# Attention with memory and a gated FFN on one core: a new hand-listed order of all work

## The chip, the cores and the metric

The kernel runs on one core of one Trainium2 chip. The metric is the device time of one execution in microseconds (us), as the median of several runs; a separate, profiled execution gives the trace. The core's engines are PE (matrix multiplication), DVE (vector), ACT (activation functions and copies with scale), POOL (a second, general vector engine) and SP, which here only issues DMA transfers. Each engine works through its own list of instructions in order, and they meet through semaphores.

## The reference

Both halves read the same tokens `x` (2048 tokens of width 512). One half is causal-style attention in four segments of 512 tokens with 32 heads of width 16, plus a linear memory that each segment reads and then adds to. The other half is a gated feed-forward network of width 1792. A gate per token mixes them.

```python
q, k, v = x @ wq, x @ wk, x @ wv            # 32 heads, 4 segments of 512
mask = (ar[:, None] < ar[None, :]) * -1e9
for s in range(4):
    p = softmax(qs @ ks.T * Dh**-0.5 + mask); a_dot = p @ vs
    a_mem = (phi(qs) @ M) / (phi(qs) @ z + 1e-6)      # phi(t) = t + 1 if t > 0 else exp(t)
    o = sigmoid(beta) * a_mem + (1 - sigmoid(beta)) * a_dot
    M, z = M + phi(ks).T @ vs, z + sum(phi(ks))
a = o @ wo
b = (gelu(x @ w_gate) * (x @ w_up)) @ w_down
g = sigmoid((x * gate_w).sum(-1))
return g * a + (1 - g) * b
```

## The kernel before

The work is cut into 1020 named tasks. A task is a run of instructions on one engine, and its name holds the segment `s` first: `K0_1` is the key product of segment 0, block 1. The names that matter here:

- `ld_...`: loads. `ld_x0_*`, `ld_x1_*`, `ld_x2_*` bring the tokens of a segment, from segment 1 on as four transposing DMAs of 128 KB, one slice of 128 of the 512 columns each. `ld_wk*`, `ld_wq*`, `ld_wv`, `ld_wg*`, `ld_wu*`, `ld_wd*`, `ld_wo` bring weights: `ld_wg0` and `ld_wg0b` are the two halves (448 KB each) of the gate weight's first seven blocks, `ld_wg1` the other seven blocks (896 KB), `ld_wu0`, `ld_wu1`, `ld_wd0`, `ld_wd1` 896 KB each, `ld_wv` 512 KB. `ld_x0_1`, `ld_wk0` and `ld_wg0b` are issued by ACT, all others by SP. `ld_beta` brings `beta` to all partitions.
- `xtr0_*`, `xev0_*`: the first 256 tokens are transposed on PE and evicted. `K`, `Q`, `V`, `G`, `U`: products (`dense`, L449; V at L499; segment 0's K at L477) of four matmuls, each group into one of four PSUM banks `psD`. A colon and a digit behind a PE task's name is its bank. `Kev`, `Qev`, `Vev`, `Gev`: their evictions, on ACT (`:a`) or DVE (`:d`). `h` multiplies U into the gelu of G. A `G` product's four matmuls take the four slices of x one after another.
- `st`, `exp`, `msk`: a fill of scores into `psX` (L602), its exp on ACT (L609), its mask on POOL (L615). There is one `psX`, so a fill waits for the exp before it. `pv` (L644) is the product with the values, `tp` and `pvp` its turning and scaling on DVE.
- `vsh` and `ktr`: DMAs on SP from SBUF to SBUF that shift values by 64 partitions and transpose keys for the memory; `mz`, `nd`, `ndp`, `otr`, `ota`, `otm`: the memory's write and read.
- `betab`, `bexp`, `gqa`, `gqb`: the gate of the heads from `beta`, on DVE, ACT, POOL, DVE. `phka`, `phkb`, `phkc`: phi of the keys on DVE, ACT, DVE.
- `out` (L735), `wev`, `wo` (L749), `oev` (L753), `dma`: the down product, the output product, their mix and the store of 128 tokens.

What stands where is set by one string, `ORDER`: it lists all tasks, and an engine's list of instructions is the tasks of that engine in the string's order. The string also picks the bank of each PE product and the engine of each eviction. Nothing is decided at run time; the semaphore waits follow from which task reads and writes what.

```python
for word in ORDER.split():
    name, _, how = word.partition(":")
    t = by[name]
    ...
    if t.opens:
        for sl, i in zip(t.slots, how):
            sl.i = int(i)
```

Some loads also wait for others by hand: `ld_wv` for `ld_x0_t3`, `ld_wg0` and `ld_wu0` for `ld_wq1`, all four `ld_x1_*` for `ld_wv`, `ld_wu1` for `ld_wg0`, `ld_x2_*` for `ld_wu1`, `ld_wo` for `ld_wu0`. `ld_wd0` waits for nothing, and `ld_wg1` for nothing when it is listed ahead of `ld_wu0`.

Of the kernel before, what the change touches and what calls it, by code (L numbers as in the profile page):

```python
# [878 lines left out]
exp1_0A st1_0B exp1_0B tp0_d20 tp0_d21 pvp0_20 tp0_d30 ota0_1 pvp0_21 tp0_d31 kpada1_3 out0_1_0:1 out0_1_1 out0_1_2 V2_0a:2 Vev2_0a:d G1_9:3 V2_1b:0
Vev2_1b:d wev0_1:d st1_0C G1_8:2 G1_10:0 G1_11:1 gelu1 gd1_9 G1_7:3 gd1_8 gd1_10 gd1_7 gd1_11 G1_13:2 gd1_13 G1_12:0 gd1_12 phqc1_2 phkc1_0 mzq0  # L880
pvp0_31 pvp0_30 ota0_3 V2_0b:3 Vev2_0b:d ota0_2 V2_1a:1 Vev2_1a:d out0_0_0:2 out0_0_1 out0_0_2 nd1_0:0 ndp1_0 phkc1_2 exp1_0C st1_0D exp1_0D K2_0:3
K2_2:1 wev0_0:d Kev2_0:d Kev2_2:a K2_1:0 st1_0E Kev2_1:d U1_2:2 h1_2 wo0_1:1 nd1_3:3 nd1_1:0 exp1_0E st1_1A ld_x3_2 vsh1_00 vsh2_01 ktr1_1 ktr1_0
oev0_1 ndp1_1 wo0_0:2 oev0_0 kpada2_0 vsh1_21 out0_2_0:1 nd1_2:0 msk1_0C msk1_0A exp1_1A st1_1B exp1_1B msk1_0B gz1 msk1_0E msk1_1A msk1_0D msk1_1B
out0_2_1 wo0_2:2 ndp1_2 st1_1C exp1_1C nd1_5:0 out0_2_2 ndp1_3 wev0_2:a ndp1_5 out0_3_0:3 st1_1D nd1_4:0 out0_3_1 out0_3_2 ktr1_2 dma0 vsh1_01 otr1_3
ndp1_4 otr1_0 oev0_2 phka2_0 msk1_1C wev0_3:d ktr1_3 dma1 vsh2_00 otr1_1 ld_x3_1 ld_x3_0 ld_x3_3 exp1_1D st1_2A exp1_2A gr1 msk1_1D pv1_1:1023 st1_2B
exp1_2B tp1_d01 tp1_d00 kpadb1_3 V2_2b:0 Vev2_2b:d K2_3:1 Kev2_3:a G2_3:0 pvp1_00 Gev2_3:d tp1_d10 st1_2C U1_8:1 G2_1:0 otr1_2 V2_3a:2 h1_8 Gev2_1:d
Vev2_3a:d kpadb2_0 kpadb2_1 exp1_2C st1_2D phkb2_0 exp1_2D G2_6:1 wo0_3:0 U1_3:2 pvp1_01 tp1_d11 Gev2_6:a h1_3 phka2_2 oev0_3 st1_2E U1_0:3 V2_3b:1
G2_0:2 Gev2_0:d h1_0 Vev2_3b:d exp1_2E phkb2_2 st1_3A mz1:0 G2_4:2 G2_5:3 pvp1_10 mza1 Gev2_5:d exp1_3A st1_3B exp1_3B Gev2_4:d U1_11:1 G2_2:0
Gev2_2:d ota1_0 U1_13:3 h1_13 U1_10:2 h1_10 h1_11 G2_11:0 G2_10:3 pvp1_11 phkc2_0 phkc2_2 ota1_1 otm1_0 otm1_1 G2_12:2 G2_9:1 st1_3C gelu2 gd2_11
gd2_12 G2_7:0 G2_13:2 gd2_10 gd2_9 gd2_7 gd2_13 G2_8:3 gd2_8 U1_7:1 U2_9:0 K3_0:2 h1_7 U2_5:3 Q3_0:1 phqa2_0 h2_9 h2_5 Qev3_0:d Kev3_0:d exp1_3C  # L890
st1_3D exp1_3D U1_1:0 U2_12:3 msk1_3A msk1_2A msk1_3B U2_13:1 h2_12 h1_1 h2_13 kpada2_1 st2_0A U1_9:2 V2_2a:3 U2_7:0 msk1_2D msk1_2B msk1_2E h1_9
Vev2_2a:d vsh2_20 dma2 dma3 ktr2_0 ktr2_2 vsh2_21 exp2_0A phqb2_0 msk1_3D msk1_2C msk1_3C st2_0B h2_7 kpada2_2 pv1_3:1230 tp1_d21 exp2_0B tp1_d20
V3_1a:2 Vev3_1a:a st2_0C exp2_0C pvp1_21 tp1_d31 U1_6:1 Q3_1:2 V3_0a:0 st2_0D h1_6 pvp1_20 Vev3_0a:d Qev3_1:a V3_2b:1 U1_4:2 U1_5:0 exp2_0D st2_0E
exp2_0E tp1_d30 phqc2_0 h1_5 h1_4 ota1_2 Vev3_2b:a U1_12:3 h1_12 pvp1_31 pvp1_30 out1_1_0:0 st2_1A V3_1b:2 out1_1_1 V3_3a:3 exp2_1A st2_1B msk2_0B
msk2_0D Vev3_3a:a exp2_1B out1_1_2 U2_4:1 msk2_0E goa1 gob1 kpadb2_3 kpada2_3 msk2_0C msk2_0A msk2_1A ota1_3 h2_4 otm1_2 otm1_3 K3_1:3 mzq1 Vev3_1b:a
wev1_1:a st2_1C msk2_1B goc1 U2_1:2 Q3_3:1 V3_0b:0 Kev3_1:d kpada3_0 h2_1 Qev3_3:d kpadb2_2 exp2_1C msk2_1C st2_1D V3_2a:3 U2_6:2 exp2_1D Vev3_2a:a
wo1_1:1 Vev3_0b:d kpadb3_0 h2_6 oev1_1 st2_2A msk2_1D pv2_1:0231 exp2_2A st2_2B exp2_2B tp2_d00 pvp2_00 phqa2_2 tp2_d01 tp2_d10 pvp2_10 pvp2_01
tp2_d11 out1_0_0:0 out1_0_1 st2_2C phqb2_2 out1_0_2 V3_3b:2 Vev3_3b:d wev1_0:d out1_3_0:3 phqc2_2 pvp2_11 exp2_2C st2_2D exp2_2D wo1_0:1 out1_3_1
# [46 lines left out]
```

## Time and profile before

| what | value |
|---|---|
| time, median of 3 runs | 263.54 us (263.52 to 266.09) |
| the profiled execution's own time | 263.46 us |
| its span, from first to last instruction | 261.7 us |
| PE busy | 257.5 us, 2849 matmuls |
| DVE, ACT, POOL busy | 198.0, 203.2, 98.4 us |
| weight loads on PE (PEld) busy | 122.1 us |
| moved by DMA | 16.50 MB |

The profile is a page about one execution, with views behind it. The time is 1.76 us more than the span, which is what lies around the instructions. A matmul's busy time in the profile runs to a modelled end and overlaps the next one's, so starts one after another tell more than busy time. "Idle before" is time in which an engine stood still ahead of an instruction, with what ended it. DMA shares are means over the core's 16 DMA engines, and may stand above 1 where packets wait in flight.

### The profile page before, as it was taken

The numbers are of one execution on the slowest core, as the hardware profiler recorded it, in microseconds if no ns is written. First come the engines' busy times: TensorE is split into PE (matmuls) and PEld (weight loads), VectorE is DVE, ScalarE is ACT, GpSimd is POOL, SyncE is SP. The second block draws the span as 40 slices with busy tenths as digits, with TensorE's granted clock in tenths as the row PEclk, the third lists the DMA queues.
The fourth block names the chain that finished last, engine by engine and source line by source line (L and its number), as shares of the span: only waits on it lengthen the run. The fifth ranks groups of instructions, "written<-read, shape, count | busy, mean of one in ns | idle before, by whom it ended". The sixth has DMA issues, their size and how long they took to land.

```text
span 261.7 us, 6706 instructions
## 1 busy us (share of the span) xinstructions
PE 257.5 (98%) x2849; PEld 122.1 (47%) x2849; DVE 198.0 (76%) x412; ACT 203.2 (78%) x171; POOL 98.4 (38%) x163
## 2 busy tenths in 40 slices
...
DMA packets 31990, 16.50 MB, mean 63 GB/s; under 512 B 21592, under 2 KB 31960, under 8 KB 31960
## 3 DMA queue, kind: packets, MB, share of 16 engines
...
HBM read 7.87 MB, written 2.10 MB: 38 GB/s over the span
## 4 chain that ended last, share of the span: by engine, by line
PE 98%; DVE 0%; issue 0%; DVEq 0%
PE psD L449 48%; PE psD L735 19%; PE psX L602 9%; PE psD L644 6%; PE psD L499 6%; PE psD L749 5%; PE psD L477 1%; PE psD L547 1%; PE psD L383 1%; PE psD L577 1%; DVE xT L795 0%; DVE ost L753 0%; PE psX L786 0%; DVEq L818 0%; PE psD L769 0%
## 5 line engine op out<-in xcount | busy, mean ns | idle before, releaser
L609 ACT ACTIVATE pt<-psX 128x2048 bf16<-128x2048 f32 x72 | 135.1, 1877 | 28.3 <-PE psX L602 26.8
L615 POOL TENSOR_TENSOR pt<-pt,ctri 128x256 bf16<-128x256 bf16 x128 | 91.8, 727 | 129.2 <-ACT pt L609 124.7
L449 PE MATMUL psD<-xT,wu 128*128 128x512 bf16 x224 | 54.6, 380 | 0.0
L449 PE MATMUL psD<-xT,wg 128*128 128x512 bf16 x224 | 53.4, 379 | 0.0
L735 PE MATMUL psD<-wd,gb 128*128 128x512 bf16 x224 | 53.2, 380 | 0.0
L720 DVE TENSOR_TENSOR gb<-psD,gb 128x512 bf16<-128x512 f32 x56 | 37.2, 681 | 10.8 <-PE psD L449 10.7
L449 PEld LDWEIGHTS psD<-xT,wg 128*128 128x128 bf16 x224 | 20.8, 98 | 24.7 <-issue 1.3
L735 PEld LDWEIGHTS psD<-wd,gb 128*128 128x128 bf16 x224 | 20.7, 98 | 24.3 <-issue 2.1
L449 PEld LDWEIGHTS psD<-xT,wu 128*128 128x128 bf16 x224 | 20.2, 98 | 24.7 <-issue 2.6
L602 PE MATMUL psX<-qT,kD 32*128 32x192 bf16 (+7 forms) x512 | 28.6, 287 | 0.0
L530 DVE STREAM_TRANSPOSE tT<-psD 128x512 f32<-128x512 f32 x32 | 21.8, 701 | 5.4 <-PE psD L644 4.9
L443 DVE CAST gb<-psD 128x512 bf16<-128x512 f32 x20 | 13.6, 688 | 13.0 <-PE psD L449 13.0
L602 PEld LDWEIGHTS psX<-qT,kD 32*128 32x128 bf16 x512 | 8.2, 92 | 25.1 <-ACT pt L609 13.6
L499 PE MATMUL psD<-wv,xT 128*128 128x257 bf16 (+1 forms) x128 | 18.2, 273 | 0.0
L753 DVE SCALAR_TENSOR_TENSOR ost<-psD,gtok,wds 128x512 bf16<-128x512 f32 (+1 forms) x17 | 11.9, 711 | 7.7 <-PE psD L749 7.6
L668 DVE SCALAR_TENSOR_TENSOR ob<-tT,gq,rc 128x256 bf16<-128x256 f32 x32 | 16.7, 522 | 1.1
L703 ACT ACTIVATE gb<-psD 128x512 bf16<-128x512 f32 x28 | 15.0, 594 | 3.3 <-PE psD L449 3.2
L644 PE MATMUL psD<-pt,vsh 64*17 64x192 bf16 (+7 forms) x512 | 17.1, 283 | 0.0
L644 PE MATMUL psD<-pt,vnat 64*17 64x192 bf16 (+7 forms) x512 | 17.1, 283 | 0.0
L449 PE MATMUL psD<-xT,wq 128*128 128x512 bf16 x64 | 16.3, 379 | 0.0
L749 PE MATMUL psD<-wo,oT 128*128 128x512 bf16 (+1 forms) x68 | 16.1, 367 | 0.0
L499 PEld LDWEIGHTS psD<-wv,xT 128*128 128x128 bf16 x128 | 11.8, 97 | 6.6 <-issue 1.3
...
## 6 DMA issues: line engine op xcount, KB each, us to landing
...
wu<-in_B_w_up_dram SPq DMA_DIRECT2D x2, 896.0 KB, 8.5
wd<-in_B_w_down_dram SPq DMA_DIRECT2D x2, 896.0 KB, 6.4
vsh<-vnat SPq DMA_DIRECT2D x16, 68.0 KB, 2.7
wg<-in_B_w_gate_dram SPq DMA_DIRECT2D x1, 896.0 KB, 5.3
wq<-in_A_wq_dram SPq DMA_DIRECT2D x2, 256.0 KB, 3.5
wv<-in_A_wv_dram SPq DMA_DIRECT2D x1, 512.0 KB, 4.3
wo<-in_A_wo_dram SPq DMA_DIRECT2D x1, 512.0 KB, 4.5
```

What stands on the lines that cost most here:

```text
L449: one(name, PE, n * T_MM, [I(lambda e, i=i: e.matmul(BK[sl.i][:, :], lhs(i), rhs(i), start=(i == 0), stop=(i == n - 1)), reads(i), [bk(sl) ...
L499: one(f"V{s}_{m}{'ab'[hf]}", PE, 2 * T_MM, [I(lambda e, i=i, sl=sl, a=a, z=z, xs=xs: e.matmul(BK[sl.i][:, 0:z - a], xs(i), wv[:, i, a:z], ...
L530: one(f"tp{name}", DVE, 0.605, [I(lambda e, sl=sl, ti=ti: e.transpose(tT[ti][:, :], BK[sl.i][:, :]), [bk(sl)], [("tT", ti)])], bias=bias)
L602: ins.append(I(lambda e, t=t, kb=kb, ncol=ncol, c0=c0, g=g: e.matmul(XALL[:, g * 512 + c0:g * 512 + c0 + ncol], kD[(4 * s + t) % R_KD][32 ...
L609: one(f"exp{s}_{name}", ACT, 2048 * 0.000833 + 0.05, [I(lambda e: e.activation(pt[slot][:, :, :], xin, ACTF.Exp, scale=ATT_SCALE), [("X",) ...
L615: ins.append(I(lambda e, mv=mv: e.tensor_tensor(mv, mv, cm, ALU.mult), [("pt", slot), ("causal",)], [("pt", slot)]))
L644: ins.append(I(lambda e, kb=kb, slot=slot, c0=c0, n=n, g=g, r0=r0, sl=banks[j], va=va: e.matmul(BK[sl.i][32 * g:32 * g + 17, 64 * kb:512], ...
L668: I(lambda e, ti=ti, ri=ri, t=t, j=j, dst=dst: e.scalar_tensor_tensor(out=dst, in0=t_rows(ti), scalar=gq[:, 2 * t + j:2 * t + j + 1], in1= ...
L703: t = one(f"gd{s}_{ft}", ACT, 0.485, [I(lambda e, gi=gi, f=f, sl=sl: e.activation(gb[gi][:, f, :], BK[sl.i][:, :], ACTF.Gelu_apprx_tanh), ...
L720: one(f"h{s}_{ft}", DVE, 0.605, [I(lambda e, sl=sl, gi=gi, f=f: e.tensor_tensor(gb[gi][:, f, :], BK[sl.i][:, :], gb[gi][:, f, :], ALU.mult ...
L735: mm.append(I(lambda e, fb=fb, gi=gi, f=f, q=q, sl=sl: e.matmul(BK[sl.i][:, :], gb[gi][:, f, q], wd[:, fb, :], start=(fb == 0), stop=(fb = ...
L749: one(f"wo{s}_{qt}{sfx}", PE, 4 * T_MM * w / 512, [I(lambda e, kb=kb, q=q, so=so, c=c, w=w: e.matmul(BK[so.i][:, 0:w], oT[:, kb, q], wo[:, ...
```

## The change

`ORDER` is replaced as a whole. All 1020 tasks, their instructions and their sizes stay; new are places, banks, and for a few evictions the engine. On SP the loads of `ld_wd0` and `ld_wg1` move up: `ld_wd0` from behind `ld_wd1` to directly behind `ld_wv`, and `ld_wg1` to directly behind `ld_wg0`, both ahead of the four `ld_x1_*`. The first gate product `G0_6` stands four PE groups further back: `Q0_2`, `V0_2b`, `V0_0a` and the fill `st0_0C` now stand ahead of it. `G0_5` moves up ahead of `G1_6`, and `V1_2b`, which was the first reader of segment 1's tokens, behind it. `xev0_1` moves from DVE to ACT. Of the diff, the first pv and all ahead of it, and the end:

```diff
-ld_x0_0 ld_wk1 ld_x0_1 warm1:0 ident xtr0_1 xev0_1:d xtr0_0 warm2 xev0_0:d vones0 masks ld_wk0 causal1 gwz ld_x0_t2 ld_x0_t3 ld_wq0 ld_wq1 ld_gw
-causal0 consts K0_1a:1 K0_3a:2 K0_3b K0_2a:3 K0_0a:0 K0_2b K0_0b K0_1b K0_0c K0_2c K0_3c K0_1c Kev0_0:d Kev0_2:d kpadb0_0 kpadb0_2 causal kpada0_0
-Kev0_3:a Q0_0:0 ld_wg0b Qev0_0:a Q0_1:3 st0_0A gwtr:2 Kev0_1:d gwev Q0_3:0 ld_wv ld_wg0 Qev0_1:d V0_1b:1 V0_3a:2 V0_3b:3 exp0_0A Qev0_3:d Vev0_3a:a
-Vev0_1b:a st0_0B Vev0_3b:d kpada0_2 kpada0_1 V0_0b:0 V0_1a:2 V0_2a:1 Vev0_0b:d G0_6:3 Gev0_6:d Vev0_1a:d Vev0_2a:d exp0_0B st0_0C exp0_0C Q0_2:0
-G0_2:3 V0_2b:2 ld_x1_2 ld_x1_1 ld_x1_3 ld_x1_0 ld_beta st0_0D Vev0_2b:a exp0_0D Gev0_2:d kpadb0_1 Qev0_2:d phka0_0 V1_2b:1 V0_0a:3 G1_6:2 V1_0b:0
-Vev1_2b:d phka0_2 st0_0E Vev0_0a:d Vev1_0b:d G0_1:1 Gev1_6:a exp0_0E Gev0_1:d Q1_2:3 V1_3b:2 V1_3a:0 kpada0_3 Qev1_2:d Vev1_3a:d phkb0_2 phkc0_2
-Vev1_3b:d st0_1A gz0 exp0_1A gr0 Q1_0:1 V1_0a:3 G1_5:0 Vev1_0a:d Gev1_5:d st0_1B Q1_1:2 K1_0:3 exp0_1B phkb0_0 ld_wu1 ld_x2_0 G0_5:0 Qev1_0:d kpadb0_3
-vsh0_21 st0_1C exp0_1C Qev1_1:d ld_x2_1 ld_x2_3 ktr0_3 ld_wg1 Gev0_5:d V1_2a:1 K1_3:2 K1_1:0 vsh0_01 Vev1_2a:a vsh0_20 ld_x2_2 ktr0_2 vsh0_00 ld_wd1
-st0_1D phkc0_0 betab Kev1_1:d kpada1_1 G0_4:1 G0_3:0 Gev0_4:d Kev1_0:d Gev0_3:d Kev1_3:a ld_wd0 ld_wu0 ktr0_1 ktr0_0 vsh1_20 ld_wo V1_1a:2 Vev1_1a:d
-exp0_1D bexp st0_2A exp0_2A msk0_0B msk0_0D msk0_0C kpada1_0 msk0_0E goa0 gob0 msk0_0A msk0_1A msk0_1C msk0_1D gqa gfull msk0_1B G0_0:1 Q1_3:3 G1_1:0
-Qev1_3:d phqa1_0 st0_2B Gev0_0:d gqb Gev1_1:a pv0_1:2301 exp0_2B tp0_d01 tp0_d00 pvp0_01 Q2_0:3 Qev2_0:d tp0_d11 st0_2C K1_2:2 Kev1_2:d pvp0_00
-tp0_d10 gelu0 G0_8:3 G0_13:1 gd0_13 G0_10:2 G0_11:0 G0_9:1 gd0_8 gd0_10 gd0_9 gd0_11 G0_12:3 G0_7:2 gd0_12 G1_2:1 U0_0:0 gd0_7 Gev1_2:d pvp0_11 h0_0
-U0_13:3 U0_10:2 h0_10 Q2_1:1 Qev2_1:d exp0_2C st0_2D mz0:0 U0_7:2 U0_9:1 pvp0_10 h0_13 exp0_2D phqb1_0 st0_2E exp0_2E phka1_0 h0_7 mza0 h0_9 ota0_0
...
-ndp3_5 oev2_2 ndp3_4 ota3_1 dma11 otr3_2 otr3_1 otr3_3 otr3_0 pv3_3:1203 tp3_d20 tp3_d21 pvp3_20 pvp3_21 tp3_d30 tp3_d31 ota3_2 pvp3_31 pvp3_30 otm3_1
-otm3_0 ota3_3 out3_0_0:1 out3_2_0:2 out3_0_1 out3_2_1 out3_3_0:0 out3_0_2 out3_3_1 wev3_0:a otm3_2 otm3_3 wo3_0:3 dma10 oev3_0 dma12 wo3_1:1 out3_2_2
-out3_3_2 wo3_2:3 oev3_1 wev3_2:a oev3_2 wo3_3b:1 dma13 dma14 wev3_3:a oev3_3b dma15b wo3_3a:2 oev3_3a dma15a
+ld_x0_0 ld_x0_1 warm1:0 ident xtr0_1 masks ld_wk1 ld_x0_t2 ld_x0_t3 ld_wq0 ld_wk0 causal0 xtr0_0 xev0_0:d xev0_1:a
+warm2 K0_1a:1 K0_1b gwz ld_wq1 ld_gw consts K0_2a:2 K0_0a:3 K0_0b K0_3a:0 K0_3b K0_0c K0_2b K0_1c K0_2c K0_3c Kev0_0:d
+kpadb0_0 Kev0_1:d Q0_0:3 Kev0_3:d Kev0_2:a ld_wg0b Qev0_0:a phka0_0 kpada0_0 gwtr:1 Q0_1:2 st0_0A exp0_0A Q0_3:0
+kpada0_2 Qev0_1:d kpadb0_1 kpada0_1 gwev ld_wv ld_wd0 V0_2a:3 V0_0a:2 V0_1a:1 ld_wg0 Qev0_3:d vones0 Vev0_0a:d
+Vev0_1a:d kpadb0_2 st0_0B exp0_0B V0_1b:0 Vev0_1b:d Vev0_2a:a ld_wg1 V0_2b:2 Q0_2:1 V0_0b:0 Vev0_2b:d Vev0_0b:d
+ld_x1_1 ld_x1_0 ld_x1_2 st0_0C V0_3b:2 V0_3a:3 Qev0_2:d Vev0_3b:d gz0 Vev0_3a:d G0_6:0 Gev0_6:d G0_2:1 Gev0_2:d
+exp0_0C st0_0D G0_5:2 gr0 ld_x1_3 vsh0_01 ld_beta phkb0_0 G1_6:3 V1_2b:0 exp0_0D Gev1_6:a st0_0E exp0_0E phkc0_0
+phka0_2 Vev1_2b:d causal1 goa0 causal Q1_2:1 V1_3a:3 Qev1_2:a G0_1:0 kpadb0_3 Vev1_3a:d Gev0_5:d st0_1A exp0_1A
+phkb0_2 V1_0b:3 betab gob0 Vev1_0b:d kpada0_3 Gev0_1:d Q1_0:1 Qev1_0:d bexp G1_5:2 V1_0a:3 Vev1_0a:d msk0_0D msk0_0B
+msk0_0A st0_1B msk0_1A gfull gqa Q1_1:0 V1_3b:1 Qev1_1:d Vev1_3b:d K1_0:3 exp0_1B st0_1C exp0_1C msk0_0E msk0_1B
+msk0_0C V1_2a:0 K1_1:1 Vev1_2a:a Kev1_1:a Kev1_0:d phkc0_2 K1_3:3 Kev1_3:d Gev1_5:d vsh0_20 ld_wu1 ld_x2_2 ld_x2_3
+ld_x2_0 st0_1D V1_1a:0 G0_3:1 G0_4:3 exp0_1D st0_2A exp0_2A msk0_1C goc0 msk0_1D Gev0_4:d Gev0_3:d Q1_3:2 G0_0:3
+G1_1:1 Qev1_3:d gqb Vev1_1a:d Gev0_0:a st0_2B ktr0_3 vsh0_00 vsh1_21 vsh0_21 ld_x2_1 ktr0_1 Gev1_1:d ld_wu0 ktr0_0
+ktr0_2 ld_wo ld_wd1 kpada1_0 pv0_1:2031 exp0_2B tp0_d01 Q2_0:0 tp0_d00 pvp0_01 Qev2_0:d K1_2:2 Kev1_2:d tp0_d11
+G0_10:0 G0_13:2 G0_8:1 pvp0_00 tp0_d10 gelu0 gd0_8 gd0_13 gd0_10 st0_2C G0_12:3 G0_11:1 G0_9:2 G0_7:0 gd0_12 gd0_11
+gd0_9 gd0_7 Q2_1:3 U0_0:1 U0_13:2 ota0_0 pvp0_10 h0_0 phka1_2 G1_2:0 U0_10:1 exp0_2C st0_2D h0_13 phqa1_2 kpadb1_1
+mz0:2 Gev1_2:d h0_10 phka1_0 kpadb1_0 Qev2_1:a U0_7:3 U0_9:0 exp0_2D phkb1_2 st0_2E exp0_2E h0_9 mza0 U0_1:1 V1_1b:0
+G1_4:2 h0_7 Gev1_4:d st0_3A Vev1_1b:a exp0_3A G1_0:3 Q2_2:0 U0_5:2 phqa1_0 kpadb1_2 phkb1_0 Gev1_0:d st0_3B Qev2_2:a
+exp0_3B mzq0 h0_5 pvp0_11 ota0_1 h0_1 U0_11:3 h0_11 msk0_2A gz1 msk0_2E msk0_2D phqb1_0 U0_4:0 h0_4 U0_12:2 phqc1_0
+h0_12 st0_3C exp0_3C gr1 phqb1_2 U0_6:1 U0_2:3 G1_3:0 st0_3D Q2_3:2 h0_2 h0_6 U0_3:3 Gev1_3:d Qev2_3:d h0_3 U0_8:1
...
+pv3_3:0132 tp3_d20 tp3_d21 pvp3_20 otr3_3 dma11 pvp3_21 otr3_1 tp3_d30 tp3_d31 pvp3_30 ota3_2 pvp3_31 out3_2_0:0
+out3_0_0:1 out3_0_1 out3_2_1 out3_0_2 out3_3_0:3 out3_3_1 wev3_0:a otr3_0 otr3_2 otm3_0 otm3_1 ota3_3 otm3_2 otm3_3
+wo3_0:2 dma10 oev3_0 dma12 wo3_1:1 out3_2_2 oev3_1 out3_3_2 wo3_2:2 wo3_3a:1 wev3_2:d oev3_2 dma13 dma14 wo3_3b:0
+wev3_3:a oev3_3a dma15a oev3_3b dma15b
```

More of the change, by code (lines that the diff above doesn't have):

```diff
@@ L879 @@
[L879 to L898, printed above, removed]
@@ new lines @@
+out0_0_1 out0_0_2 gd1_12 exp1_0C st1_0D exp1_0D Vev2_0b:d wev0_0:a K2_0:0 Kev2_0:d kpada1_2 K2_1:2 Kev2_1:a K2_2:3
+vsh1_01 vsh2_00 Kev2_2:d st1_0E exp1_0E nd1_1:0 wo0_1:1 U1_2:2 nd1_3:3 ndp1_1 oev0_1 h1_2 st1_1A wo0_0:0 out0_2_0:1
+nd1_2:2 kpada1_3 ndp1_2 oev0_0 ndp1_3 exp1_1A st1_1B exp1_1B ld_x3_3 ktr1_1 ktr1_0 ktr1_2 ld_x3_2 vsh1_20 dma0 ktr1_3
+vsh1_00 msk1_0E msk1_0A msk1_1A msk1_0D ld_x3_0 out0_2_1 wo0_2:2 msk1_0C msk1_1B st1_1C exp1_1C nd1_5:0 ndp1_5 otr1_3
+ld_x3_1 out0_2_2 out0_3_0:3 wev0_2:d st1_1D out0_3_1 nd1_4:0 out0_3_2 oev0_2 kpadb2_1 ndp1_4 msk1_1C dma1 otr1_2
```

56 lines of the change are left out of this document (39 added, 17 removed).

## The prediction, made before the changed kernel was run

> **What bounds the kernel now.** I read the page first, then the chain that ended last in order of time, then the waits.
>
> ```profile
> span 261.7 us, 6706 instructions
> PE 257.5 (98%) x2849; PEld 122.1 (47%) x2849; DVE 198.0 (76%) x412; ACT 203.2 (78%) x171; POOL 98.4 (38%) x163
> PE 98%; DVE 0%; issue 0%; DVEq 0%
> ```
>
> ```profile
> 4.45 0.77 DVE xT L795 x2
> 5.31 3.65 PE psD L477 x32
> ...
> 15.08 0.97 PE psD L449 x4
> ...
> 19.97 0.86 PE psD L449 x4
> ...
> 41.90 11.33 PE psD L449 x52
> ...
> 256.99 0.88 PE psD L749 x4
> 257.95 0.60 issue
> ```
>
> ```profile
> PEld psX L602 <- ACT pt L609: 13.6, 38, 0.4
> ...
> PE psD L383 <- PEq L930: 0.8, 1, 0.8
> ...
> PE psD L477 <- DVE xT L795: 0.4, 1, 0.4
> ```
>
> The whole chain from 5.31 to 257.9 is PE. The 52 products at 41.90 take 11.33 us, 0.218 us each, and a group of four takes 0.86 wherever it stands; it takes 0.97 when a fill follows (the group at 15.08). The matmuls themselves wait twice in the whole run, 0.8 us for the start and 0.4 us at the first key product. The other waits are those of weight loads, 0.4 us at the longest, under matmuls that run on. So between 5.31 and 257.9 there is no hole for a new order to fill: what it can win lies in the first 5.3 us, in the last 3.8, and in the 0.1 us steps ahead of fills. What it can lose is every wait that it opens on PE, in full, because PE has no slack later to make it up.
>
> **The head, the tail and the steps.** `K0_1a`, the first key product, needs `xev0_1` and `ld_wk1`.
>
> ```profile
> 1.25 0.41 SPq L341 DMA_DIRECT2D wk<-in_A_wk_dram  x1
> ...
> 6.46 0.39 SPq L341 DMA_DIRECT2D wv<-in_A_wv_dram  x1
> 8.52 0.37 SPq L341 DMA_DIRECT2D wg<-in_B_w_gate_dram  x1
> 10.82 5.54 SPq L345 DMA_TRANSPOSE xT<-in_A_x_dram  x4
> 16.41 0.58 SPq L341 DMA_DIRECT2D omem<-in_A_beta_dram  x1
> 17.03 0.43 SPq L341 DMA_DIRECT2D wu<-in_B_w_up_dram  x1
> ```
>
> ```profile
> wv<-in_A_wv_dram SPq DMA_DIRECT2D x1, 512.0 KB, 4.3
> ...
> wk<-in_A_wk_dram SPq DMA_DIRECT2D x1, 256.0 KB, 3.9
> ```
>
> The weight lands at 1.25 + 3.9 = 5.15, later than the first of the two evictions (half of 0.77 after 4.45, so 4.84); the profile puts the wait down to DVE, whose second eviction ends at 5.22. SP's list starts as before, so `K0_1a` stays at 5.3 with `xev0_1` on ACT: I take nothing. If DVE were what it waits for, two evictions side by side would be worth up to 0.4. The tail keeps its PE order but for the two halves of the last product, and I take nothing there. Of 72 fills, 69 stood behind something other than a `pv`; in the new order it is 68 (`st1_3B` now follows `mz1`), so one step of 0.1 us goes: -0.1.
>
> **The loads, which are the change that can cost.** In PE's list `G0_6` has four more groups ahead of it, and `G1_6` has `G0_5` ahead of it instead of `V1_2b`.
>
> ```profile
> 15.03 1.02 PE L449 MATMUL psD<-xT,wg 128*128 128x512 bf16 x4
> ...
> 18.92 1.05 PE L499 MATMUL psD<-wv,xT 128*128 128x257 bf16 x8
> 19.81 1.02 PE L449 MATMUL psD<-xT,wg 128*128 128x512 bf16 x4
> ```
>
> `G0_6` moves from 15.03 by a product (0.87), two V groups (0.44 each) and a fill (0.33) to 17.1. `G1_6` moves from 19.81 by 0.86 - 0.44 to 20.2, and becomes the first reader of segment 1's tokens; its fourth matmul, with the last slice, stands at 20.2 + 0.65 = 20.9.
>
> Behind `ld_wv` the DMA queues now hold `ld_wd0`, `ld_wg0`, `ld_wg0b` and `ld_wg1` ahead of the four slices: 896 + 448 + 448 + 896 KB = 2.75 MB, where there were 0.92. The same amount, three loads of 896 KB, goes through in one piece later in this trace.
>
> ```profile
> 8.00:10.20 2.20, 2.20 (x16) 1.40 (x15) 2.20 (x7) 0.93 (x2) 0.00 (x0) 1.00 0.79 235
> ...
> 36.00:44.40 8.40, 8.40 (x170) 3.99 (x169) 6.96 (x17) 7.46 (x5) 4.30 (x8) 1.00 0.98 327
> 44.40:46.50 2.10, 2.10 (x11) 0.98 (x10) 0.63 (x1) 2.10 (x4) 0.00 (x0) 1.00 1.63 112
> ...
> 12.00:13.40 1.40, 1.40 (x17) 1.05 (x18) 0.72 (x2) 1.40 (x3) 0.00 (x0) 1.00 1.27 362
> 13.40:14.80 1.40, 1.40 (x19) 1.08 (x12) 1.38 (x6) 1.33 (x3) 0.00 (x0) 1.00 1.47 42
> ```
>
> ```profile
> L345 SPq DMA_TRANSPOSE xT<-in_A_x_dram x4: 1168/1258/1736, 10.8 to 15.1; - x4
> DMA to landing us min/median/max: 2.5/3.9/4.7
> ```
>
> ```profile
> wu<-in_B_w_up_dram SPq DMA_DIRECT2D x1, 896.0 KB, 10.5
> ...
> phkt<-phk SPq DMA_TRANSPOSE x2, 9.5
> ```
>
> The last two columns of the windows are DMA share and GB/s. At 235 GB/s the stretch to 10.20 carries the 0.52 MB of `ld_wv`. The stretch from 36.00 carries the three loads in 8.4 us at 327 GB/s, and what was issued behind them waited: the last load landed 10.5 us after issue, the two transposes 9.5 in the middle, against 2.5 for a slice with a free queue. So I take one queue in order of issue. `ld_wg0`: 1.83 MB from 10.2 at 327 is 5.6 us, so 15.8, before 17.1: no wait, by 1.3 us. `ld_wg1` is through at 10.2 + 8.4 = 18.6. The slices then need what they needed before from 14.80, when the queue moved again, to the last landing at 15.1 + 2.5 = 17.6: 2.8 us. That is 21.4, against 20.9: **0.5 us of wait** at `G1_6`. Bounds: at 362 GB/s, the loads' own rate from 12.00, they are through at 17.8 and the slices at 20.6, no wait. With a collapse as from 13.40 (42 GB/s for 1.4 us, just where transposes followed loads) it is 22.8, a wait of 1.9. The same collapse stands at 44.40, where transposes again followed a load. I take 0.5, because the row at 36.00 is the nearest: same queue, same bytes, though two of its three loads were of `w_down`, and here it is one.
>
> By the Trainium skill (DMA: Bandwidth & Descriptors, Latency and other measured facts) a DMA transpose was measured at 261 GB/s with a non-contiguous middle dimension. By this figure, an estimate, the slices' 0.52 MB would take 2.0 us instead of 2.8, `G1_6` would not wait, and the sum would be 263.6. Here 2.8 was measured from the queue's restart, so the trace differs and the sum goes by it.
>
> Behind a waiting `G1_6` stand all of PE's groups, and ACT and DVE have nothing else that is due; the whole program shifts. SP's later work moves too.
>
> ```profile
> omem<-in_A_beta_dram SPq DMA_DIRECT2D x1, 8.0 KB, 4.8
> ...
> vsh<-vnat SPq DMA_DIRECT2D x16, 68.0 KB, 2.7
> ...
> 38.48 2.08 PE psD L644 x128
> ```
>
> `ld_beta` landed at 16.41 + 4.8 = 21.2, 3.6 after the last slice; now that is 25.0. `betab` waits for it on DVE, where its turn comes at about 24.4 (behind the evictions of `V1_3a` and `G0_5`), and behind it stand `Vev1_0b` and `Gev0_1`, whose banks PE wants at 26.7 and 27.5: one microsecond of it is covered, and I take nothing. `ld_wu1` and the three `ld_x2_*` right behind it come some 3 us later than before, and SP then waits until about 32 for `phkc0_2`, which now stands behind `Kev1_0` on DVE. Past that, a transpose and three copies bring `vsh0_21` to an issue near 34.4 and a landing at 37.1, with `pv0_1` at 38.4: nothing taken, 0.5 if it is late. What `ld_wd0` and `ld_wg1` leave free around 35 to 46 hides under products that did not wait, so it wins nothing.
>
> **Evictions and banks.** DVE and ACT have 24% and 22% free, and the order keeps about the old distances. The shortest re-uses of a bank become one group, as for `G0_10` behind `Qev2_0` and `G0_13` behind `Kev1_2`.
>
> ```profile
> 15.99 0.40 PE L602 MATMUL psX<-qT,kD 32*128 32x384 bf16 x8
> ...
> 16.09 0.69 DVE L443 CAST gb<-psD 128x512 bf16<-128x512 f32 x1 [1.32 <-PE psD L449]
> ```
>
> An eviction ends at 16.78, 0.79 us after the next group began at 15.99. One group of 0.86 covers that when DVE is free, and misses by up to 0.6 when another cast stands ahead. I take 0.1 for each, 0.2 in all, with 0 and 1.2 as ends.
>
> **Sum**, on the profiled execution: 263.46 - 0.1 + 0.5 + 0.2 = **264.1**. That execution is within 0.1 of the median of the runs, 263.54. A measurement here tells about 1% (2.6 us) from no change, so this is no change.
>
> **Rivals.** *No new wait.* The slices come at 362 GB/s and the banks fit: 263.46 - 0.1 = 263.4. For it speaks that no matmul waits in the old order with distances that are much the same; against it, that the two loads ahead of the slices are new.
>
> *Slower: the slices behind the loads.* The place is `G1_6`. If the collapse strikes twice while 2.75 MB and the slices go through, as it did twice in the first 47 us (13.40 and 44.40, 1.4 and 2.1 us), the last slice lands at 21.4 + 3.5 = 24.9, and PE waits 4.0 us instead of 0.5: 263.46 - 0.1 + 4.0 + 0.2 = 267.6. It decides from a landing after 23.6 on (20.9 + 2.7). Against it: three loads in a row ran through 8.4 us without a collapse.
>
> *Faster.* The order may do more than the bound that I read. By the Trainium skill (Perfetto Trace Analysis, Identifying the Most-Contended Engine), PE's headroom is judged by weight-load busy time and not by matmul busy time. The weight loads are 47% here, which reads as room. Working it out from rows: if the head lost the 0.4 us before 5.31, the tail the 0.60 of issue and every one of the 68 steps its 0.1 us, the gain would be 7.8: 255.7. But the steps stand between kinds of product, not at waits, and the products at 41.90 show no room.
>
> *It does not do what it says.* An order found with the landings of the old order of loads does not know that the slices now come later; that is the forecast's own 0.5, and has no chance of its own.
>
> **How the numbers follow.** Forecast 0.58, its own range 263.4 to 265.8 (0 to 1.9 at `G1_6`, 0 to 0.5 elsewhere). No new wait 0.26. Slower by over 1%, above 266.2: 0.14. Faster by over 1%: 0.02. Within 1% is 0.58 + 0.26 = 0.84. The range 263.2 to 266.3 leaves some 0.13 above and 0.05 below.
>
> **What would show it.** PE busy without a wait from 5.3 to about 20; a wait of about half a microsecond in the gate product of segment 1 near 20, released by a DMA of x; slices that land 5 us or more after issue, one after another near 21; no wait at `G0_6`; the loads in one stretch from 10 to 18 at over 300 GB/s. It is wrong if `G0_6` waits, if PE waits more than 2.6 us in all, or if the time falls under 262.5, which would mean room on PE that I do not see.

## The result and the profile after

The new order takes 265.4 us in the median of 22 runs (263.81 to 266.38); the kernel before, beside it on the same chip, 264.1 (263.47 to 266.09). The ratio is 1.0046, 95% interval 1.0033 to 1.006: 1.2 us slower, by less than the 1% from which this document calls a time changed. The profiled execution took 265.11 us, 1.65 more than the one of before.

The head of the page, and the chain's shares by engine:

```profile
span 263.4 us, 6671 instructions
...
PE 254.9 (97%) x2816; PEld 121.5 (46%) x2849; DVE 198.6 (75%) x412; ACT 202.9 (77%) x171; POOL 97.1 (37%) x163
...
PE 83%; DVE 7%; DMA 4%; SPq 3%; issue 2%; DVEq 0%
```

33 matmul records are missing, so the 254.9 is not to be compared with 257.5. What can be read is that the chain, 98% PE before, is now only 83% PE. Some of that is bookkeeping (it now runs through DVE work that is as long as PE's beside it), but DMA and SPq are new: PE has waited for transfers. The waits of PE's matmuls and then of its weight loads (total, times, longest):

```profile
PE psD L449 <- issue: 1.2, 7, 0.2
PE psD L644 <- issue: 1.0, 1, 1.0
...
PE psD L477 <- ACT xT L794: 0.2, 1, 0.2
```

```profile
PEld psD L644 <- issue: 2.5, 6, 1.2
...
PEld psD L449 <- DMA xT<-in_A_x_dram: 1.3, 3, 0.5
```

Two places stand out. One was forecast: the weight loads of a gate product wait for slices of x, three times. The other was not: inside a `pv` (L644) PE stands for 1 us once, and the releaser is "issue", which means that nothing in the profile held it.

I set every PE group's start in both traces against one count of the same durations without stalls. The difference of 1.65 us splits into: -0.2 by an earlier head, +0.55 around `G1_6`, +1.28 inside `pv2_3`, -0.1 for the fill step that went, +0.2 in pieces of 0.1 (banks), -0.1 behind PE's end. So the forecast's own terms (-0.1 + 0.5 + 0.2) came out, and three quarters of the loss is a term that the sum did not have.

**The loads.** Windows of the new order (last three columns: granted clock, DMA share, GB/s), and the slices of x1 (the issue's own duration, min/median/max; then issue to landing):

```profile
10.20:16.80 6.60, 6.60 (x62) 4.01 (x61) 5.20 (x18) 4.77 (x5) 0.00 (x0) 1.00 1.07 376
16.80:18.90 2.10, 2.05 (x18) 0.87 (x16) 1.57 (x6) 2.10 (x3) 0.79 (x4) 1.00 1.70 114
18.90:21.00 2.10, 2.02 (x15) 0.52 (x7) 2.07 (x3) 1.98 (x2) 0.00 (x0) 1.00 1.10 210
```

```profile
L345 SPq DMA_TRANSPOSE xT<-in_A_x_dram x4: 1154/2175/2725, 10.6 to 16.8; - x4
...
DMA to landing us min/median/max: 4.2/7.2/9.0
```

The loads go at 376 GB/s up to 16.8, then the rate falls to 114 for 2.1 us as the transposes begin, then they run at 210. The last slice lands at 21.05; `G1_6` begins at 20.12, and its four matmuls start at 20.12, 20.34, 20.57 and 21.10 instead of 0.22 apart.

**The stall in `pv2_3`.** PE's weight loads there, in order of time (start, us, what, idle time before and its releaser):

```profile
187.60 0.12 PEld L602 LDWEIGHTS psX<-qT,kD 32*128 32x128 bf16 x8 [0.42 <-ACT gb L442]
187.93 0.09 PEld L644 LDWEIGHTS psD<-pt,vnat 64*17 64x17 bf16 x4 [0.21 <-POOL pt L615]
...
189.73 0.08 PEld L644 LDWEIGHTS psD<-pt,vsh 64*17 64x17 bf16 x1
191.05 0.09 PEld L644 LDWEIGHTS psD<-pt,vsh 64*17 64x17 bf16 x3 [1.23 <-issue]
```

125 of the 128 weight loads go in 1.8 us; then the last three, and the last four matmuls with them, come only after a stop of 1.23 us, in the middle of a run of four alike. In the trace of before the same place runs through:

```profile
189.31 0.11 PEld L644 LDWEIGHTS psD<-pt,vsh 64*17 64x17 bf16 x4
189.59 0.55 PEld L449 LDWEIGHTS psD<-xT,wk 128*128 128x128 bf16 x4 [0.17 <-DVE tT L530]
```

The late ones read the same `pt` and `vsh` and write the same bank as the one before them, so no semaphore can stand between them. What PE can lack there is the instructions. PE's own program comes by DMA too. The queues in a window of 2 us around the start of that `pv`:

```profile
DMA packets 254, 0.17 MB, mean 85 GB/s; under 512 B 133, under 2 KB 253, under 8 KB 253
...
q8 instruction: 1, 0.02, 5.0%
```

That window is 187 to 189; the one from 186 to 188 holds no packet at all. The packet of q8 is 16 KB, it runs from 188.23 to 189.82, and over the whole run q8 carries 22 of them, 0.36 MB, for PE's 2849 weight loads and 2849 matmuls: 259 instructions a packet. `pv2_3` is 128 of each, 256 instructions in 2.1 us, so it uses up about one packet. In the trace of before the same fetch ran at 185.70, 1.8 us ahead of `pv2_3` and not 0.3 behind its start.

By the Trainium skill (Runtime: NRT & Kernel Launch, Instruction fetch mechanics) each engine's program is refilled in blocks of 16 KiB, 256 instructions, by a queue of the sequencer's own while the current block runs, and the cost of a boundary is mostly hidden. The trace agrees on the blocks (22 of 16 KB); it does not agree that the cost is hidden where 256 instructions are used up in 2.1 us.

### The profile page after: what moved, and what is told of

The parts are those of the page before. It is cut to its first block, busy times and chain, and to the rows that moved or that the text cites. A ratio compares the mean times of both kernels' runs of the same rounds, so it can differ in the third digit from the quotient of the medians.

```text
span 263.4 us, 6671 instructions
## 1 busy us (share of the span) xinstructions
PE 254.9 (97%) x2816; PEld 121.5 (46%) x2849; DVE 198.6 (75%) x412; ACT 202.9 (77%) x171; POOL 97.1 (37%) x163
## 2 busy tenths in 40 slices
DMA packets 31990, 16.50 MB, mean 63 GB/s; under 512 B 21592, under 2 KB 31960, under 8 KB 31960
## 4 chain that ended last, share of the span: by engine, by line
PE 83%; DVE 7%; DMA 4%; SPq 3%; issue 2%; DVEq 0%
PE psD L449 42%; PE psD L735 17%; PE psX L602 8%; PE psD L644 6%; PE psD L749 5%; PE psD L499 4%; DMA xT<-in_A_x_dram 3%; SPq L345 2%; DMA wv<-in_A_wv_dram 2%; DVE gb L720 1%; DVE omem L561 1%; DVE tT L530 1%; DVE gb L443 1%; PE psD L547 1%; DVE ost L753 1%
## 5 line engine op out<-in xcount | busy, mean ns | idle before, releaser
L615 POOL TENSOR_TENSOR pt<-pt,ctri 128x256 bf16<-128x256 bf16 x128 | 89.7, 712 | 94.3 <-ACT pt L609 85.4
L449 PE MATMUL psD<-xT,wu 128*128 128x512 bf16 x214 | 53.3, 380 | 1.1 <-issue 0.8
L449 PE MATMUL psD<-xT,wg 128*128 128x512 bf16 x218 | 52.6, 380 | 0.6 <-DVE gb L443 0.2
L735 PE MATMUL psD<-wd,gb 128*128 128x512 bf16 x216 | 51.7, 379 | 1.1 <-issue 0.6
L443 DVE CAST gb<-psD 128x512 bf16<-128x512 f32 x22 | 15.0, 684 | 4.8 <-PE psD L449 4.8
L499 PE MATMUL psD<-wv,xT 128*128 128x256 bf16 (+1 forms) x128 | 18.4, 273 | 0.0
L644 PE MATMUL psD<-pt,vsh 64*17 64x192 bf16 (+7 forms) x512 | 17.2, 283 | 1.0 <-issue 1.0
L668 DVE SCALAR_TENSOR_TENSOR ob<-tT,gq,rc 128x256 bf16<-128x256 f32 x32 | 16.8, 525 | 1.1
L644 PE MATMUL psD<-pt,vnat 64*17 64x192 bf16 (+7 forms) x512 | 17.1, 283 | 0.0
L428 POOL TENSOR_SCALAR gz<-gzr 128x4 f32<-128x4 f32 x4 | 1.0, 261 | 40.8 <-ACT gzr L507 28.0
L449 PE MATMUL psD<-xT,wq 128*128 128x512 bf16 x61 | 15.7, 380 | 0.3 <-issue 0.2
(82 smaller groups left out, 266.3 us busy)
```

Source lines behind the costliest of these rows:

```text
L443: (DVE, 0.60, [I(lambda e: e.tensor_copy(dst, src()), [bk(sl), *reads], writes)]),
L449: one(name, PE, n * T_MM, [I(lambda e, i=i: e.matmul(BK[sl.i][:, :], lhs(i), rhs(i), start=(i == 0), stop=(i == n - 1)), reads(i), [bk(sl) ...
L499: one(f"V{s}_{m}{'ab'[hf]}", PE, 2 * T_MM, [I(lambda e, i=i, sl=sl, a=a, z=z, xs=xs: e.matmul(BK[sl.i][:, 0:z - a], xs(i), wv[:, i, a:z], ...
L615: ins.append(I(lambda e, mv=mv: e.tensor_tensor(mv, mv, cm, ALU.mult), [("pt", slot), ("causal",)], [("pt", slot)]))
L644: ins.append(I(lambda e, kb=kb, slot=slot, c0=c0, n=n, g=g, r0=r0, sl=banks[j], va=va: e.matmul(BK[sl.i][32 * g:32 * g + 17, 64 * kb:512], ...
L668: I(lambda e, ti=ti, ri=ri, t=t, j=j, dst=dst: e.scalar_tensor_tensor(out=dst, in0=t_rows(ti), scalar=gq[:, 2 * t + j:2 * t + j + 1], in1= ...
```

## The experiments

The theory to test: (1) at `pv2_3` PE ran out of program, because the boundary of a block stands just ahead of a `pv`; (2) `G1_6` waits for x1 because `ld_wd0` and `ld_wg1` are ahead of it, and `G0_6` stands further back to pay for that; (3) the head is as it was. The rivals: a late transfer or a semaphore at `pv2_3`; loads that cost nothing; a head that wins. Ratios are against the kernel before on the same chip.

| run | time, us | ratio (95%) |
|---|---|---|
| e1 new order, two loads back | 265.37 | 1.0047 (1.0023 to 1.007) |
| e2 new order, 24 more PE instructions | 264.76 | 1.0023 (1.0004 to 1.0043) |
| e3 new order, 24 fewer | 266.16 | 1.0067 (1.0043 to 1.0092) |
| e4 = e1 and e2 | 264.9 | 1.0018 (0.9998 to 1.0039) |
| e5 order before, 8 fewer | 264.65 | 1.0034 (1.0017 to 1.0052) |
| e6 new order, 8 more | 264.08 | 1.0007 (0.9997 to 1.0018) |
| e7 order before, two loads ahead | 265.94 | 1.0077 (1.0065 to 1.0089) |
| e8 new order, `G0_6` forward | 268.99 | 1.0183 (1.0152 to 1.0214) |
| e9 new order, 8 more, two loads back | 263.83 | 1.0007 (0.9992 to 1.0022) |
| e10 new order, 8 more, `xev0_1` on DVE | 264.41 | 1.0018 (1.0006 to 1.0031) |
| e11 order before, `xev0_1` on ACT | 267.35 | 1.0127 (1.011 to 1.0144) |
| e12 order before, 8 more | 263.88 | 0.9996 (0.9985 to 1.0007) |

### The program of PE: e2, e3, e5, e6, e12

All five change one line, the number and width of the warm-up matmuls, at equal columns in all:

```diff
-    for name, n, cols in (("warm1", 45, 80), ("warm2", 7, 80)):
+    for name, n, cols in (("warm1", 57, 63), ("warm2", 7, 80)):   # e2;  e3: 33, 109
+    ...                                                           # e5: 41, 88;  e6, e12: 49, 73
```

**e2.**

> The new order with 57 warm-up matmuls of 63 columns instead of 45 of 80 (the same columns in all, 3591 against 3600): 24 more instructions on PE ahead of all else, no wait, no order and no load changed. Theory: the 1.2 us inside pv2_3 are PE without instructions, because the fetch of the next 16 KB of its program (256 instructions) is issued only as pv2_3 begins, and pv2_3 uses up 256 instructions in 2.1 us. With 24 more instructions ahead, that fetch is issued 24 instructions earlier, one to two us before pv2_3, and the stall goes: about 1.2 us less, 263.9. Rival: the stall is a semaphore wait or a late transfer that the records do not show; then it stays at 1.2 us, and the time at 265.1.

The stall is gone from the trace: no wait inside any `pv`. The time is 264.76, 0.6 less than the new order and not 1.2. The profiled execution lost 0.5 elsewhere: a matmul group at 28.6 (`Q1_1`) waited 0.42 behind DVE, which the new order itself did not show. The direction is right, the size not clean.

**e3.**

> The new order with 33 warm-up matmuls of 109 columns instead of 45 of 80 (3597 columns): 24 fewer instructions on PE ahead of all else. Theory (PE without instructions): the fetch that is issued just as pv2_3 begins now falls some 6 instructions into it, so pv2_3 still stalls, by 0.5 to 1.3 us, and the next block boundary comes to the start of pv3_1, which ran without a stall and now stands where pv2_3 stood: up to 1.2 us there as well, 265.0 to 266.3. Rival (semaphore or transfer at pv2_3): 1.2 us at pv2_3 as before, nothing at pv3_1, 265.1.

PE's matmuls at the end of `pv3_1`, and the DMA of the 3 us around it (225 to 228):

```profile
226.17 0.28 PE L644 MATMUL psD<-pt,vsh 64*17 64x256 bf16 x3
227.69 0.27 PE L644 MATMUL psD<-pt,vsh 64*17 64x256 bf16 x1 [1.24 <-issue]
```

```profile
DMA packets 1, 0.02 MB, mean 5 GB/s; under 512 B 0, under 2 KB 0, under 8 KB 0
...
q8 instruction: 1, 0.02, 2.2%
```

The stall left `pv2_3` and came up in `pv3_1`, 37 us later, where no kernel had shown one. No task was moved, so what moved the stall is the place of the block boundary. I had expected some stall to stay at `pv2_3`, and none did, so the dangerous stretch is narrower than I thought. The second fence settles a point that I had held open: the only packet on all DMA queues is the fetch itself, so it is not slowed by other traffic. It starts at 225.18, takes 1.03 us, and PE goes on at 227.69: 2.5 us from the start of the packet to the next instruction, with the queues to itself.

**e5.**

> The kernel before, not the new order, with 41 warm-up matmuls of 88 columns instead of 45 of 80 (3608 columns against 3600): 8 fewer instructions on PE ahead of all else. Theory: the stall inside pv2_3 comes from where the 256-instruction blocks of PE's program fall. In the new order the boundary is some 18 instructions ahead of pv2_3, behind the last wait for psX, in the order before some 23, ahead of that wait (five more waits stand in PE's list before pv2_3). 8 fewer move the old order's boundary to 15, and then the kernel before stalls there too, by 0.9 to 1.3 us: 264.7 to 265.4. Rival: the stall belongs to the new order (its copies and transposes around pv2_3); then the kernel before shows none and stays at 264.2.

The kernel before, with four warm-up matmuls fewer, at `pv2_3`:

```profile
189.27 0.10 PEld L644 LDWEIGHTS psD<-pt,vsh 64*17 64x17 bf16 x3
190.56 0.08 PEld L644 LDWEIGHTS psD<-pt,vsh 64*17 64x17 bf16 x1 [1.19 <-issue]
```

It stalls as the new order does, in the same run of four, now with one weight load left and not three, by 1.19 us. Its fetch ran at 188.04, behind the start of `pv2_3` (187.47). The interval of the time, 0.4 to 1.4 us, holds the stall. So a loss of this kind does not need the new order.

**e6.**

> The new order with 49 warm-up matmuls of 73 columns instead of 45 of 80 (3577 columns): 8 more instructions on PE ahead of all else, a third of what was added before. Theory: the boundary moves from 18 to 26 instructions ahead of pv2_3, ahead of the wait for psX, and the fetch is issued 1 to 2 us sooner, as in the order before: no stall, about 264.2 to 264.8. Rival (any late transfer, or time alone): 8 instructions at the head change nothing, and 0.9 to 1.3 us are lost at pv2_3, 265.4.

The new order with four more warm-up matmuls, the end of `pv2_3` and what follows; then the DMA of 185 to 187:

```profile
189.84 0.11 PEld L644 LDWEIGHTS psD<-pt,vsh 64*17 64x17 bf16 x4
190.12 0.55 PEld L449 LDWEIGHTS psD<-xT,wk 128*128 128x128 bf16 x4 [0.17 <-DVE tT L530]
```

```profile
DMA packets 97, 0.07 MB, mean 34 GB/s; under 512 B 16, under 2 KB 95, under 8 KB 95
...
q8 instruction: 1, 0.02, 3.2%
```

The last four go without a stop, and the fetch runs at 185.80, 2.4 us sooner than in the new order as it was. The time is 264.08, the same as the kernel before. Eight instructions, at the other end of the program, took back all that the change had cost in time.

**e12**, the control.

> The kernel before with 49 warm-up matmuls of 73 columns: the control for the two kernels with 8 more instructions. Theory: its block boundary at pv2_3 moves from 23 to 31 instructions ahead, still no stall, and the other warm-up costs nothing: 264.1, within 0.1% of the kernel before. Rival: the other warm-up is itself worth something (then by as much as here), or a boundary comes to the start of another pv and costs about 1.2 us there.

Ratio 0.9996: the other shape of the warm-up is worth nothing by itself, so e6's gain is the boundary.

What follows: in the new order the program runs out 7 instructions before the end of `pv2_3` (three weight loads and four matmuls), in e5 2 before it, in e3 1 before the end of `pv3_1`. Counted in the traces from PE's start (weight loads, matmuls and the semaphore instructions between them), PE stops behind instruction 4288 in the new order, in e1 and in e5, and behind 5056 in e3: exactly three blocks of 256 further. Both orders have as many matmuls ahead of `pv2_3`, and most waits ride on a weight load; as instructions of their own the new order has 4 fewer there than the old one (28 and 32), and that was enough to bring the boundary to this place. By this count the boundary lies 5 instructions ahead of `pv2_3` in the new order, 9 in the order before, 1 in e5 and 13 in e6, not the 18, 23, 15 and 26 of my expectations.

Why a few instructions move the fetch by 2 us stays open. I took it to be that PE's sequencer runs ahead of the engine but stops at a semaphore, here at the wait of `st3_0B` for `psX`. In the kernels that stall the boundary does lie behind such a wait, by 11 instructions (the new order), 15 (e5) and 19 (e3, at `st3_2B`); but before and e6, which do not stall, have it 7 and 3 behind the same wait. And the place alone does not decide: e8 below has the same number of PE instructions ahead of `pv2_3` as the new order, with the boundary in the same place, and in its trace the fetch ran at 190.75, 1.4 us ahead of `st3_0B`, and `pv2_3` went through:

```profile
194.29 0.11 PEld L644 LDWEIGHTS psD<-pt,vsh 64*17 64x17 bf16 x4
194.56 0.55 PEld L449 LDWEIGHTS psD<-xT,wk 128*128 128x128 bf16 x4 [0.17 <-DVE tT L530]
```

So the place of the boundary makes the stall possible; what else has to come together in an execution was not found.

### The loads and `G0_6`: e1, e4, e9, e7, e8

**e1.** In `ORDER`, the two loads go behind `ld_beta`:

```diff
- ld_wv ld_wd0 V0_2a:3 ...  Vev0_2a:a ld_wg1 V0_2b:2 ...  vsh0_01 ld_beta phkb0_0
+ ld_wv V0_2a:3 ...         Vev0_2a:a V0_2b:2 ...         vsh0_01 ld_beta ld_wg1 ld_wd0 phkb0_0
```

> The new order with ld_wg1 and ld_wd0 put behind ld_beta in SP's list (in the new order they stand ahead of the slices of x1); nothing else changed. Theory: the 0.55 us that PE waits at G1_6 is the price of these two loads, 1.75 MB ahead of the slices. Then the slices land 3 to 4 us sooner (by 17.5 instead of 21.05), G1_6 does not wait, and the profiled time falls by 0.5 to 0.6 from 265.1 to about 264.5; the stall of 1.2 us inside pv2_3 stays. Rival: the loads are harmless, the slices are slow because they are transposes right after ld_wg0; then G1_6 still waits 0.3 or more and the time stays within 0.2 of 265.1.

The slices of e1, and its PE where `G0_5` and `G1_6` stand:

```profile
L345 SPq DMA_TRANSPOSE xT<-in_A_x_dram x4: 1155/1262/2061, 10.4 to 15.0; - x4
...
DMA to landing us min/median/max: 3.0/4.7/5.5
```

```profile
19.68 1.90 PE L449 MATMUL psD<-xT,wg 128*128 128x512 bf16 x8
```

The slices are in by 18.04 and not 21.05, and two gate products run through: the wait is gone, so its cause is shown. The stall in `pv2_3` stayed, as expected, at 0.9 us. But the time did not fall (1.0047 against 1.0046). In the profiled execution the half microsecond went elsewhere: its key products ran partly at half speed, as those of e9 below.

**e4 and e9** are e1 with 24 and with 8 more instructions.

> The new order with both: ld_wg1 and ld_wd0 behind ld_beta, and 57 warm-up matmuls of 63 columns. Theory: the two losses add, so 0.55 + 1.2 go and what stays of the change is the gain of about 0.3 in the first 6 us and some 0.15 lost at banks: 263.3, between 0.1 and 0.4 under the kernel before on the same chip. Rival: the losses hide each other (PE waits elsewhere for what it no longer waits for here), and it stays above 264.3.

> The new order with 8 more instructions at the head (49 warm-up matmuls of 73 columns) and ld_wg1 and ld_wd0 behind ld_beta: no stall at pv2_3 and no wait at G1_6. Theory: the wait at G1_6 is worth up to 0.5 us; it is less in those executions in which the clock steps up only after the first key products, because there PE is late anyway and the slices land at the same time. So 0.2 to 0.5 less than with 8 more alone (264.08 there): 263.6 to 263.9, 0.1 to 0.2% under the kernel before, at the edge of what 5 rounds tell. Rival: the wait is already made up later and nothing is won: 264.1.

Neither trace has the wait at `G1_6` or the stall; e4 took 264.9 and not 263.3, and e9 has the same ratio as e6, 1.0007. So taking the wait away wins nothing that can be measured. The key products (duration min/median/max) and the microsecond from 6 to 7, first in the new order, then in e9:

```profile
L477 PE MATMUL psD<-xT,wk x32: 269/273/283, 4.9 to 8.5; 128*128 128x256 bf16 x32
```

```profile
6.00:7.00 1.00, 1.00 (x12) 0.90 (x10) 0.00 (x0) 0.00 (x0) 0.00 (x0) 1.00 0.94 319
```

```profile
L477 PE MATMUL psD<-xT,wk x32: 272/273/421, 5.1 to 9.3; 128*128 128x256 bf16 x32
```

```profile
6.00:7.00 1.00, 1.00 (x7) 0.74 (x6) 0.00 (x0) 0.00 (x0) 0.00 (x0) 1.00 0.95 315
```

In e9 7 matmuls run in the microsecond in which the new order runs 12, and the longest takes 421 ns instead of 283, though the granted clock reads 1.00 in both. By the first clock record of each trace PE came to full speed at 3.6 us in the new order's profile, 4.3 in that of before, 6.4 in e1, 6.6 in e4, 6.8 in e9. The key products of these last three took 0.4 to 0.6 us longer than the new order's. By the Trainium skill (TensorE: Matmul & The Clock Gate, What's actually happening) the array runs at half clock until it was busy in a window of 3.4 us that runs free, so that the moment differs from run to run; these rows agree, and in all fourteen traces the clock's changes lie whole multiples of 3.41 us apart.

In an execution with a late head PE comes late to `G1_6` as well, and the slices are there: e10 below has the loads of the new order, starts its keys at 5.70, and shows no wait for x. The head's loss and the wait do not add, the larger one counts. That fits the missing gain of e1 and e9, but how often a late head falls in the timed runs was not measured, so that part stays open.

**e7.** The kernel before with the two loads ahead:

```diff
- ld_wv ld_wg0 Qev0_1:d
+ ld_wv ld_wd0 ld_wg0 ld_wg1 Qev0_1:d
```

> The kernel before with only ld_wd0 and ld_wg1 moved ahead, to right behind ld_wv and right behind ld_wg0; PE's order as before, so G0_6 stands four groups further forward than in the new order. Theory: ld_wg0 and ld_wg0b then land near 16.7 as in the new order, G0_6, due at 15.0, waits 1.7 us, and what remains for the slices of x1 (landing near 21, first reader V1_2b due at 18.9 + 1.7) is 0.3 to 0.5 more: 2.0 to 2.3 us, 266.2 to 266.6. It would show that the four groups further back are what pays for the loads ahead. Rival: the loads would also be in time for the old place of G0_6 (my estimate was 15.8, 0.8 late): 265.0 or less.

```profile
16.14 0.38 PE L449 MATMUL psD<-xT,wg 128*128 128x512 bf16 x1
17.08 0.60 PE L449 MATMUL psD<-xT,wg 128*128 128x512 bf16 x2 [0.57 <-DMA wg<-in_B_w_gate_dram]
...
21.55 1.05 PE L499 MATMUL psD<-wv,xT 128*128 128x257 bf16 x8 [0.93 <-DMA xT<-in_A_x_dram]
```

`G0_6` waits for the gate weight and `V1_2b` for the slices; the time is 1.9 us more, 265.94, just under what I had given. So the loads ahead cost 2 us in the old order of PE.

**e8.** The new order with `G0_6` back at the front:

```diff
- Vev0_2a:a ld_wg1 V0_2b:2 ...  Vev0_3a:d G0_6:0 Gev0_6:d G0_2:1
+ Vev0_2a:a ld_wg1 G0_6:0 Gev0_6:d V0_2b:2 ...  Vev0_3a:d G0_2:1
```

> The new order with the place of G0_6 undone: G0_6 and its eviction put ahead of V0_2b, five groups further forward; the loads stay as in the new order. Theory: G0_6 is then due at about 14.2 and waits for ld_wg0 and ld_wg0b, which land at 16.5 and 16.9: 2.3 to 2.7 us. G1_6 comes that much later and no longer waits for the slices (-0.55). Net 1.8 to 2.1 us more than the new order, 267.2 to 267.5. Rival: the place of G0_6 is of no account, because the loads, not the order, decide when G1_6 can run; the two waits are the same time counted twice, and it stays within 0.5 of 265.4.

PE's longest wait, and the windows behind it (the clock is the third column from the end):

```profile
PE psD L449 <- DMA wg<-in_B_w_gate_dram: 2.1, 1, 2.1
```

```profile
16.80:18.00 1.20, 1.15 (x3) 0.27 (x4) 0.00 (x0) 0.00 (x0) 0.00 (x0) 0.55 2.34 305
18.00:19.00 1.00, 1.00 (x5) 0.55 (x4) 0.29 (x1) 0.00 (x0) 0.00 (x0) 0.50 0.55 57
19.00:20.00 1.00, 0.96 (x4) 0.50 (x4) 0.83 (x3) 0.00 (x0) 0.00 (x0) 0.50 1.18 245
20.00:21.00 1.00, 0.82 (x5) 0.52 (x5) 0.06 (x1) 0.00 (x0) 0.00 (x0) 0.83 0.78 147
```

The wait is where it was expected, 2.1 us on the matmuls where I had said 2.3 to 2.7. What I had not expected is that it costs nearly twice its length: behind it the clock stands at 0.5 for 3.4 us, and the groups `G0_6`, `V0_2b` and `Q0_2` take 1.7 us more than in the new order. The median is 268.99, 3.6 above the new order, from six runs that lie between 266.89 and 269.79; the profiled one, without the stall in `pv2_3`, took 268.43. With e7 this shows what the place of `G0_6` is for: without it the loads ahead cost 1.9 us in the old order and more in the new one.

### The head: e10, e11

**e10.** `xev0_1:a` becomes `xev0_1:d`.

> The new order with 8 more instructions at the head and xev0_1 back on DVE, ahead of xev0_0 in time as in the order before. Theory: K0_1a waits for ld_wk1 (start 0.13 us after its landing in every profile but one), not for the evictions, so the engine of xev0_1 changes nothing: 264.1, K0_1a at 4.9 to 5.4 as the weight lands. Rival: the new head wins 0.2 to 0.4 by the two evictions side by side; then this loses them, 264.3 to 264.5, with K0_1a 0.13 after the end of an eviction.

```profile
5.70 3.49 PE L477 MATMUL psD<-xT,wk 128*128 128x256 bf16 x26 [0.38 <-DVE xT L795]
```

My text had the order wrong: in the new list `xev0_0` stands ahead of `xev0_1`, so on DVE the eviction that `K0_1a` needs came second and ended at 5.65, past the weight's landing at 4.79. So in this trace the new order needs ACT, because that order turned the two evictions round. In the times it is not shown: 1.0018 against 1.0007 for e6 is 0.3 us, and the intervals overlap.

**e11.** The same the other way, in the order before.

> The kernel before with only xev0_1 on ACT instead of DVE. Theory: nothing (within 0.1 of the kernel before, 264.1), because K0_1a waits for ld_wk1. Rival: K0_1a waits for DVE, as the profile of before puts it, and starts up to 0.4 us sooner, near 4.9: 263.7.

```profile
PE psD L477 <- DMA wk<-in_A_wk_dram: 2.4, 1, 2.4
```

```profile
8.00:10.00 2.00, 1.92 (x10) 1.36 (x11) 0.00 (x0) 0.00 (x0) 0.00 (x0) 0.50 0.93 319
```

This answered another question. In the old list `ld_wk0`, which ACT issues, stands behind `xev0_1`; with the eviction on ACT the load was issued at 4.45 and not at 1.2, PE waited 2.4 us for it and then ran at half clock: 3.4 us lost. `K0_1a` itself began at 5.09, ld_wk1 having landed at 4.37 and the eviction having ended at 5.04. It says nothing on whether ACT alone would win.

No version beat the kernel before by more than the intervals.

## Why the prediction was right, and where not

- **The class and the range** were right: 264.1 forecast, no change; 265.11 in the profile and 265.4 in the median, inside 263.2 to 266.3. That the time lies inside owes something to luck: the forecast loss was 0.6 us, the profile's is 1.65, and the range held a term that the sum did not know.
- **`G1_6`, 0.5**: +0.55 in the profile, by the mechanism named, a DMA of x near 20. The last slice landed at 21.05 (21.4 forecast). e1 took the loads away and the wait went. But in the timed runs no gain of that size showed (e9 against e6, with intervals of 0.3 to 0.4 us to each side).
- **`G0_6`, no wait by 1.3**: no wait, but by less than 0.3. `ld_wg0` and `ld_wg0b` landed at 16.50 and 16.90, not 15.8; `G0_6` began at 16.78. The step that failed is "one queue in order of issue": `ld_wd0` was in at 13.17, and at the 376 GB/s that flowed up to 16.8 the 0.46 MB of `ld_wg0` behind it would have been in near 14.4, an estimate; instead it came 2 us later, and `ld_wg1` at 19.11. That fits loads that share the engines, so that bytes issued later go along with earlier ones; no run tested it.
- **The collapse** that I set as a bound (a rate of 42 GB/s as transposes follow loads) came, once, at 16.80 with 114 GB/s; the rival needed it twice.
- **The head, nothing**: right in size, and by the reason given in part of the profiles. In those of before, of e2, e5, e6 and e12 `K0_1a` starts 0.13 us after `ld_wk1` lands (5.18 and 5.31 in before, 4.73 and 4.86 in e12), although the profile puts the wait down to DVE in three of them. In the new order's own profile, as in e1, e3, e4, e8 and e9, the eviction on ACT ended after the landing (4.83 and 4.73), and `K0_1a` started some 0.05 behind it, at 4.89. So the weight decides only when it lands behind that eviction, and "every profile but one" in my text to e10 is wrong. That the new order's profile started 0.4 us sooner comes from the landing at 4.73, which before's control e12 had as well.
- **Banks, 0.2**: `G0_10` lost 0.08 and the pieces together 0.2.
- **Covered steps**: `betab` and `vsh0_21` held nobody (`vsh0_21` issued at 34.98, forecast 34.4, landed at 37.06, forecast 37.1). `ld_beta` was in at 22.48, 2.5 sooner than I had it.
- **What failed** is the sentence on which the sum rests: "What it can lose is every wait that it opens on PE". The largest loss, 1.2 us, is no wait for work or data and no term of the list. Nothing in the profile of before shows it as a cost.
